# One written list of steps replaced by another in a fused attention and gated-MLP kernel on one Trainium2 core

## The chip, the core and the metric

The kernel runs on one core of a Trainium2 chip. The profile names the engines: PE is TensorE's matmuls and PEld its weight loads, DVE is VectorE, ACT is ScalarE, POOL is GpSimd, SP is SyncE, which here issues all transfers. The metric is device time in microseconds (us); lower is better.

## What is computed

```python
# x: 2048 x 512, all bf16.  The same x feeds both branches.
xn = layernorm(x)                                  # rows, eps 1e-5
# branch A: 32 heads of 16
q, k, v = split(xn @ wqkv)                         # wqkv 512 x 1536
pq, pk  = q @ w_phi[h], k @ w_phi[h]               # 16 x 16 for each head
phi_q   = concat(softmax(pq), softmax(-pq))        # 32 features for each head; phi_k alike
kv, z   = phi_k^T v, sum over tokens of phi_k
o       = (phi_q @ kv) / (phi_q . z + 1e-6)
# branch B: F = 1792
h       = (xn @ w_gate) * (xn @ w_up)
out     = x + o @ wo + h @ w_down
```

## The kernel before

**Data.** x is taken in 16 tiles of 128 tokens, and four tiles make a group of 512. The 1792 hidden columns are 14 chunks of 128. Group 0 goes through plain matmuls. Group 1 goes through gate and up in a seven-product block scheme (Strassen's in Winograd's form) with 256 token columns (the steps with `N` before the name), and groups 2 and 3 together go through the same scheme with 512 columns. For w_down, tiles 9, 10 and 11 are paired with 13, 14 and 15 in that scheme too.

**The order of the work.** A loop builds some 1244 small closures, the steps, each with a name. At the end of the function, one string, `ORDER`, is split into words, and each word's closure is called in turn. What a closure issues is queued on its engine in that order; no scheduler changes it (`manual_schedule`). A word such as `kp7/g` gives the engine of a step that can run on several: `/v` VectorE, `/a` ScalarE, `/g` GpSimd. `SLOTS` says, for each kind of buffer, which of its places each new buffer takes, in the order in which the list asks for them: `s` is for six PSUM banks, `x` for five SBUF buffers, `e` for three exponent tiles. Where a place is asked for again, the step waits until the last reader of its former content is done.

**Turns.** `both_in_sbuf` names the steps all of whose operands are in SBUF. When such a step is called on VectorE, the next step with a GpSimd instruction gets a manual dependency on it: GpSimd waits until VectorE has done it. A VectorE step has no such wait for GpSimd (except `ws`, which waits for the last GpSimd instruction listed ahead of it).

**The steps**, with the lines that the profile shows:

- `g`, `u`: gate and up matmuls of group 0 (L351); `gc` the copy of the gate, `h` the product. `fk`, `fq` fold w_phi into the key and the query weight (L471), `fka fkv fqa fqv` copy the results; `wq` fetches the query weight transposed (L491).
- `s` statistics of a tile on VectorE, `sc` the scaling of four tiles on GpSimd, `a` the normalised tile, `xt` its transposing DMA (L523).
- `vk n.0`, `vk n.1`, `q n.0`, `q n.1`: value, key and query matmuls (L337); `vc` copies the value. `kx ky qx qy` take the exponents on ScalarE (L537), `kr qr` the sums (L549) and `ki qi` the reciprocals (L554) on VectorE, `kp qp` the product on GpSimd (L559). `kv n` adds tile n to the sum over tokens (L590), `kvm` scales that sum (L595), `qt` transposes phi_q by DMA (L616).
- `ab n`: numerators and denominators of the attention (L627); `de` the denominator (L638 on ScalarE), `rd` its reciprocal (L649), `ot` the quotient (L654), `oT` its transposing DMA (L660).
- `f n.i`: products of w_down for tile n (L678; the last two, i = 7 and 8, are with `wo`), `fs` the sum with x, `fo` the store; tile 12 is done in two parts, `f12` and `F12`.
- `n g.k`: a bound on the weights' size on ScalarE (L710); `wr wf wp ws` make powers of two of it; `up` scales the weights with these (L359); `t k i` (L774) and `z i`, `Nz i` (L796) are the differences and sums of weights and tokens that the block scheme needs.
- `p m.b` (L824): the seven products of block b; `k` keeps a partial product (L357), `j` and `d4` join them (`d4` is the direct one), `m` multiplies gate and up (L846).
- `S` (L930), `ct cb wt` (L910): sums for w_down's scheme; `P` its products (L960), `K A B` what is kept and added, `J` the joins (L989), `X t` the store of tile t (L1015).
- `=k`, `=ab`, `=f`, `=ab2` open and close two PSUM banks outside the ring: for the sum over tokens, for the attention, for the narrow blocks (`bank_f`), and for the attention of the last tiles. A pool opens when the last reader of the former one is done.

Of the kernel before, what the change touches and what calls it, by code (L numbers as in the profile page):

```python
# [50 lines left out]
Nk3.2/a j3.2 p2.4 j2.4 p7.3 Np5.2 Np4.2 p2.5 p2.6 k3.3/a Nd4.2/a qi8 j7.3 n2.0 qp8/g Nj7.2 Nm7.1/g p1.5 Np1.3
Nk1.3/a qr13 p3.3 Np3.2 k1.5/a Nj3.2 Np6.3 p6.4 p6.5 Nk2.3/a Np7.3 j2.5 m2.5/g k2.4/a m7.3/v j3.3 Np5.3 Nk3.3/a
up50/a Nj7.3 p7.4 Np2.3 Np4.3 Nd4.3 p5.4 Np3.3 Nm7.3/g Nj2.3 k3.4/a Np1.4 Nk1.4/a p4.3 j7.4 Np2.4 Np6.4 k2.5/a
t23/g Nj3.3 qi13 t30/g Nm2.3/g Nk2.4/a p3.4 j3.4 p7.5 Np7.4 Np1.5 Nj2.4 n2.1 p4.4 d4.3 Nm3.3/v Nk3.4/a t31/v
Np2.5 q10.0 Np4.4 m3.3/g k3.5/a Nk1.5/a p5.5 p4.5 Np6.5 Nj2.5 qi9 j7.5 Nm2.5/g t32/g d4.4/a Nd4.4/a Np5.4 Nj7.4
p1.6 Nk2.5/a Np7.5 Nk3.5/a q10.1 t33/v d4.5 Np3.4 wr2 Nj3.4 wf2 k1.6/a p3.5 Np4.5 up51/a Nd4.5 p6.6 Np1.6
Nk1.6/a Np2.6 qx10 j2.6 k2.6/a qp9/g j3.5 Np5.5 Nj7.5 m7.5/v m3.5/v t40/v t41/g q12.0 p5.6 Np6.6 q12.1 p7.6
Nk2.6/a Np3.5 Np7.6 Nj2.6 Nj3.5 qy10 wp2 qp13/g k3.6/a p1.7 p1.8 Nk3.6/a qx12 k1.7/a Np5.6 Np4.6 p2.7 j7.6 p3.6
p4.6 Nm7.5/g Nd4.6/a oT4 qr10 Nj7.6 Np1.7 qy12 p2.8 p6.7 Np3.6 k1.8/a Nk1.7/a j3.6 k2.7/a Np6.7 j2.7 Nk2.7/a
d4.6/a q14.0 q14.1 Np7.7 Nj3.6 j2.8 Np2.7 p7.7 Nk3.7/a qx14 Np2.9 Nm3.5/v m2.7/v t42/v Nj2.7 k3.7/a Np4.7 qy14  # L60
Np5.7 Nd4.7 p5.7 Nj7.7 t43/g Np2.8 Np1.8 p4.7 Np3.7 j7.7 Nm2.7/g Nm7.7/v Nj3.7 Nm3.7/v Nk1.8/a Np6.8 Nk2.8/a
p1.9 d4.7 p3.7 k1.9/a Np7.8 Np5.8 p6.8 m7.7/g qt13 fo3 qt8 j3.7 p2.9 Nk3.8/a Np4.8 Nd4.8/a k2.8/a p1.10 Nj7.8
Nj2.8 Np3.8 m3.7/g Np1.9 j2.9 Nk1.9/a k1.10/a t50/v ws2 Nj3.8 S1.0/g p6.9 p2.10 Nj2.9 j2.10 Np6.9 p7.8 Np5.9
p5.8 k2.9/a m2.9/v p7.9 Nk2.9/a t52/v k3.8/a j7.8 Np7.9 Nk3.9/a t51/g p5.9 p1.11 p4.8 Nj7.9 p3.8 k3.9/a p4.9
t53/g p6.10 Np4.9 Np3.9 Nm2.9/v j7.9 d4.8/a j3.8 m7.9/g qi10 k1.11/a Nd4.9 p6.11 p3.9 Nj3.9 up61/a t60/v d4.9
Nm7.9/g qp10/g k2.10/a Np1.11 p2.11 j3.9 p7.10 k2.11/a k3.10/a j2.11 Np1.10 p5.10 j7.10 Nm3.9/g m2.11/g m3.9/v
Np2.10 Np2.11 Nk1.10/a Nj2.10 p4.10 p7.11 k3.11/a q15.0 q15.1 S0.3/v qy15 Nk1.11/a d4.10/v p4.11 p3.10 p5.11
Np6.10 qx15 Nk2.10/a p1.12 Nj2.11 Nm2.11/g j3.10 Np6.11 j7.11 t61/g t62/g t63/g Np2.12 Np7.10 p2.12 f6.3 d4.11
m7.11/g k1.12/a oT7 j2.12 Nk3.10/a Np4.10 Nk2.11/a Nd4.10/a f6.1 p3.11 f6.4 qr12 Np7.11 Np5.10 p1.13 ct2.2/a
Nk3.11/a Nj7.10 j3.11 p6.12 fo1 Np3.10 k2.12/a f7.0 Np4.11 k1.13/a p2.13 Nj3.10 S0.5/v j2.13 f7.4 Np1.12 f7.1  # L70
p7.12 cb11.1/a p6.13 Nk1.12/v Nd4.11 Np5.11 f6.8 qi12 Nj7.11 Nj2.12 S1.3/g S2.4/g m3.11/v k3.12/a S0.4/g S1.4/g
Np6.12 q11.0 f6.7 Nk2.12/a ct2.1/a Np7.12 Np3.11 p5.12 qr14 Nj3.11 Nk3.12/a j7.12 Nm3.11/g qp12/g Np4.12 p4.12
Np1.13 q11.1 p3.12 d4.12/a Nd4.12/a m2.13/v Nk1.13/a Np2.13 f7.2 Np5.12 f6.2 Np6.13 f7.8 k2.13/a qr15 j3.12
p7.13 Nj2.13 Nk2.13/a ct1.0/a qi14 Nj7.12 inv1 cb11.0/v qx11 k3.13/a p5.13 Np7.13 f4.2 f4.5 Np3.12 f4.1 Nk3.13/a
p4.13 wt1.0/v Nm2.13/v Nj3.12 Nm7.11/v Np5.13 f7.7 f6.0 qt9 Np4.13 j7.13 qp14/g Nj7.13 Np3.13 d4.13 Nd4.13 p3.13
f4.3 Nj3.13 =ab2 ab8 qy11 ct2.3/g S0.1/v de8/v rd8 ot8 qi15 f4.7 f6.5 f5.2 Nm3.13/g f4.4 f5.0 ct2.0/g ab9 f7.5
S0.2/v Nm7.13/v S2.6/g de9/a rd9 ot9 S2.2/v S2.3/v F12.3 f6.6 f4.8 F12.1 f7.6 wt2.0/v S1.1/g S1.5/g qt14 qt10
qp15/g qt12 m7.13/v oT8 f4.0 j3.13 f7.3 f4.6 F12.2 f5.8 fs4 fs6 ab14 f5.7 de14/a ct1.1/a rd14 oT9 fo0 ot14
S0.6/v m3.13/v f5.1 f5.4 qr11 qi11 f8.8 oT14 f12.5 F12.6 f8.3 fs7 f5.5 f5.3 F12.5 f12.2 ab12 f8.2 P1b.10 de12/a
wt1.1/g wt2.2/g P1a.10 f5.6 f8.7 cb21.0/a f8.5 f8.4 F12.0 K1.10/v S2.1/v rd12 ot12 f12.6 qt15 fo6 P1a.11 f12.1  # L80
ab13 f12.4 P1b.11 oT12 qp11/g fs5 fo7 fo4 fo5 qt11 wt2.1/g ct3.0/a de13/a rd13 ot13 S1.2/v cb22.1/v S1.6/v f8.0
P1a.9 f12.0 P1b.9 f8.1 S3.0/v wt2.3/v S2.5/v wt4.1/v oT13 f12.3 F12.7 f12.7 f12.8 S3.6/v fs12 K1.11/a S2.0/v
ab10 F12.8 ct3.1/a F12.4 cb21.1/a de10/a K1.9/a A1.9/v wt3.1/v P6a.10 f8.6 wt4.0/g P6a.9 P6b.9 K6.9/a cb22.0/a
A6.9/g S3.5/g wt4.3/g S3.4/g P6a.11 P5a.10 P5b.10 Fs12 P6b.10 K6.10/a P2a.9 P2w.9 K5.10/a fs8 P5a.9 rd10 ot10
# [1026 lines left out]
```

## Time and profile before

| | us |
|---|---|
| median of 3 runs | 214.34 (214.32 to 215.28) |
| the profiled execution's own time | 215.05 |
| its span | 213.3 |

A row of the stretches gives, after the stretch and its length, the busy time (us) of TensorE's matmuls, its weight loads, VectorE, ScalarE and GpSimd, each with its count of instructions, then the granted clock, the DMA engines' mean busy share and GB/s. A row of the timeline gives the start, the duration, the engine, the line, the operation with out<-in, the shape, how many instructions are taken together, and in brackets the idle time ahead and what ended it. A matmul of 512 columns is shown with 0.38 us, but such matmuls follow one another every 0.216 us. The mean granted clock of the span is 0.998.

### The profile page before, as it was taken

What the parts mean: (1) busy time and instruction counts of PE and PEld (TensorE: products, weight loads), DVE (VectorE), ACT (ScalarE), POOL (GpSimd) and SP (SyncE); (2) the same over time, 40 slices, a digit from 0 to 9 for tenths busy, and PEclk for the clock granted to TensorE, in tenths of its full rate; (3) what the DMA queues carried; (4) which work ended last, traced back from release to release, by engine and by line L of the source; (5) the groups of instructions that cost most, each with busy time, mean ns of one, the idle gap of its engine ahead of it and who ended that gap; (6) DMA issues with size and microseconds to landing.
All of it is one profiled execution on the core that took longest, in us unless ns stands there. A gap on an engine that the chain in (4) does not pass through costs nothing.

```text
span 213.3 us, 4174 instructions
## 1 busy us (share of the span) xinstructions
PE 206.5 (97%) x1452; PEld 117.8 (55%) x1452; DVE 185.3 (87%) x372; ACT 153.2 (72%) x296; POOL 149.8 (70%) x146
## 2 busy tenths in 40 slices
...
GB/s 158 260 274 383 379 297 177 92 8 33 70 25 77 0 68 105 147 103 77 0 3 0 0 3 32 179 13 3 0 0 0 0 130 119 101 148 75 50 78 74
DMA packets 47253, 19.95 MB, mean 94 GB/s; under 512 B 37504, under 2 KB 46976, under 8 KB 47104
## 3 DMA queue, kind: packets, MB, share of 16 engines
...
q8 instruction: 11, 0.18, 0.4%
q14 instruction: 10, 0.08, 0.2%
HBM read 8.67 MB, written 2.10 MB: 50 GB/s over the span
## 4 chain that ended last, share of the span: by engine, by line
PE 78%; DMA 9%; DVE 6%; SPq 2%; ACT 1%; POOL 1%; issue 1%; DVEq 0%; ACTq 0%; POOLq 0%
PE sa L824 16%; PE fin L678 15%; PE sc L824 9%; PE k L337 5%; PE q L337 5%; PE da L960 5%; PE pv L337 4%; PE sb L824 4%; DMA wT<-in_A_wqkv_dram 3%; PE u L351 3%; DMA wgu<-in_B_w_up_dram 2%; PE g L351 2%; DMA oT<-otok 2%; PE db L960 2%; PE dd L960 2%; PE dc L960 2%
## 5 line engine op out<-in xcount | busy, mean ns | idle before, releaser
L549 DVE TENSOR_REDUCE sums<-e 128x64 f32<-128x1024 f32 x32 | 38.3, 1198 | 3.0 <-ACT e L537 2.9
L559 POOL TENSOR_TENSOR phik<-e,rs 128x1024 bf16<-128x1024 f32 x16 | 30.8, 1935 | 13.8 <-DVE rs L554 10.4
L678 PE MATMUL fin<-wd,hT 128*128 128x512 bf16 (+2 forms) x154 | 37.1, 359 | 0.0
L559 POOL TENSOR_TENSOR phiq<-e,rs 128x1024 bf16<-128x1024 f32 x16 | 31.5, 1975 | 4.8 <-DVE hT L846 2.7
L824 PEld LDWEIGHTS <-T 128*128 128x128 f16 x224 | 21.9, 98 | 17.4 <-issue 0.5
L846 POOL TENSOR_TENSOR hT<-u_sb,hT 128x256 f16<-128x256 bf16 (+1 forms) x23 | 21.1, 920 | 5.3 <-DVE T L774 3.0
L357 ACT COPY k<-sa 128x512 f32<-128x512 f32 (+1 forms) x42 | 19.5, 483 | 5.6 <-PE sa L824 4.1
L359 ACT ACTIVATE k<-sa 128x512 f32<-128x512 f32 (+1 forms) x41 | 19.7, 494 | 4.9 <-PE sa L824 4.2
L824 PEld LDWEIGHTS <-wgu 128*128 128x128 bf16 x168 | 16.3, 98 | 12.3
L337 PEld LDWEIGHTS <-x 128*128 128x128 f16 x144 | 13.4, 98 | 14.4 <-DMA x<-xn 1.1
L678 PEld LDWEIGHTS <-hT 128*128 128x128 f16 (+1 forms) x154 | 14.0, 98 | 11.8
L337 PE MATMUL pv<-vk,x 128*128 128x512 bf16 x48 | 18.2, 379 | 0.8 <-DMA x<-xn 0.8
L351 PEld LDWEIGHTS <-wgu 128*128 128x128 bf16 x128 | 12.0, 98 | 12.0 <-DMA wgu<-in_B_w_up_dram 0.4
L554 DVE RECIPROCAL rs<-sums 128x64 f32<-128x64 f32 x32 | 17.3, 543 | 1.5
L337 PE MATMUL k<-vk,x 128*128 128x512 bf16 x48 | 18.2, 379 | 0.0
L824 PE MATMUL sa<-ss,T 128*128 128x512 f16 x56 | 16.3, 379 | 0.0
L839 DVE SCALAR_TENSOR_TENSOR hT<-sc,k 128x512 f16<-128x512 f32 (+1 forms) x28 | 15.3, 548 | 1.1 <-PE sc L824 0.9
L359 ACT ACTIVATE wgu<-wgu,up 128x1024 bf16<-128x1024 bf16 x14 | 16.0, 1152 | 0.0
L710 ACT ACTIVATE junk<-wgu 128x1024 bf16<-128x1024 bf16 x14 | 15.0, 1077 | 1.2 <-DMA wgu<-in_B_w_gate_dram 1.2
L843 DVE TENSOR_TENSOR u_sb<-sc,k 128x512 bf16<-128x512 f32 (+1 forms) x28 | 15.0, 545 | 0.6 <-PE sc L824 0.5
L537 ACT ACTIVATE e<-q 128x512 f32<-128x512 f32 x24 | 13.9, 601 | 1.9 <-POOL phik L559 1.4
L351 PE MATMUL u<-xnT,wgu 128*128 128x512 bf16 (+1 forms) x64 | 14.6, 352 | 0.1
...
## 6 DMA issues: line engine op xcount, KB each, us to landing
out_dram<-o_sb SPq DMA_DIRECT2D x15, 128.0 KB, 1.9
...
xall<-in_A_x_dram SPq DMA_DIRECT2D x1, 1024.0 KB, 12.1
xall<-in_A_x_dram SPq DMA_DIRECT2D x4, 128.0 KB, 2.5
...
```

Of the source, the lines that this page charges most:

```text
L337: nc.tensor.matmul(ps, lhsT=xt(n)[:, j, :], rhs=w[:, j, :], start=(j == 0), stop=(j == DC - 1))
L351: nc.tensor.matmul(ps, lhsT=w[:, c, f * P:(f + 1) * P], rhs=xnT[:, c, lo:hi], start=(c == 0), stop=(c == DC - 1))
L357: A.copy(out=dst, in_=src)
L359: A.activation(out=dst, in_=src, func=AF.Identity, scale=scale)
L549: V.tensor_reduce(out=sums[:], in_=ev(), axis=AX.X, op=ALU.add)
L554: V.reciprocal(out=rs[:].rearrange("p a b -> p (a b)"), in_=held.pop((s + "s", n))[:])
L559: eng.tensor_tensor(out=phi[:].rearrange("p g (x f) -> p (g x) f", f=DH), in0=ev(), in1=held.pop((s + "i", n))[:].to_broadcast((P, 2 * H, ...
L678: nc.tensor.matmul(held["fin", n, lo], lhsT=l, rhs=r, start=len(done) == 1, stop=len(done) == FC + DC)
L824: nc.tensor.matmul(mine[bankname], lhsT=ww[:, j, :], rhs=xx[:, j, :], start=start and j == 0, stop=(j == hc - 1), skip_group_check=True)
L839: V.scalar_tensor_tensor(out=h(*to), in0=mine[ps], scalar=gate_scale, in1=mine[kept][:], op0=ALU.mult, op1=ALU.add)
L846: eng.tensor_tensor(out=h(*to), in0=mine["u", i][:], in1=h(*to), op=ALU.mult)
L960: nc.tensor.matmul(mine[ps][:, 0:W], lhsT=l, rhs=r, start=bool(mine.pop((ps, "new"), False)), stop=True, skip_group_check=True)
```

## The change

`ORDER` and `SLOTS` are replaced. The new list has the same steps, but that the stores of tiles 13, 14 and 15 come in two halves (`X13.0`, `X13.1` and so on). 96 of the 1244 steps have another engine; among them ten `t` go from VectorE to GpSimd and five the other way, `z1` and `Nz2` from GpSimd to VectorE, four `de` from ScalarE to VectorE, and `de6` and `de8` the other way. By the change's description, each VectorE step on SBUF operands is now listed behind its GpSimd step. The code around it takes a few more general forms (`KN`, a scale for `gate_copy`, another source for `half`), which with `KN = 7` give the same instructions.

The diff, cut to the lists' beginnings and ends and the code:

```diff
 ORDER = """
-g3 gc3/a =k g1 gc1/a fk2 fk0 g0 u3 fkv2/v fkv0/v fka2/a fka0/a k1 ky1 kx1 u0 gc0/v h3 k0 u1 k2 h0 kr1 h1 ki1 kx0
-ky0 kr0 s6 s5 ky2 n1.0 g4 g6 gc4/a u6 g7 n0.5 kx2 gc6/a gc7/a s7 k3 kp1/g s4 sc4 kx3 n1.6 n0.6 ky3 u7 h7 h6 a5/g
-xt5 u4 g12 g11 g13 h4 ki0 u12 g9 u13 a6/g kp0/g gc11/a s9 s11 s10 s8 u11 a4/a xt4 n0.3 gc9/a kr2 gc13/a n0.1 h11
-h13 xt6 wq g10 gc10/a gc12/a kr3 n2.4 u9 h9 ki2 kv0 g5 sc8 a11/g a10/g vk5.0 a8/g xt11 ki3 vk5.1 kp2/g a9/a
-gc5/a a7/a vc5/a s13 h12 kx5 vk4.0 vk4.1 vc4/a kp3/g vk6.0 s14 fq0 xt10 s15 s12 sc12 xt8 xt9 xt7 ky4 kx4 ky5
-fqa0/v vk6.1 ky6 kv1 g2 fq2 kv2 kx6 kr4 ki4 kr6 ki6 fqv0/a fqv2/a kp4/g u5 kv3 vk7.0 vk7.1 kr5 kp6/g vc6/a gc2/a
-n1.3 fqa2/a ky7 vk8.0 vk8.1 kv4 kx7 ki5 h5 u2 kr7 ki7 n1.4 kp5/g vc8/a kx8 ky8 a12/a vk10.0 vk10.1 vc7/a ky10
-kx10 a13/a kp7/g h2 vk9.0 kv5 kr8 ki8 kp8/g kv6 xt12 vk9.1 ky9 vc10/a kx9 n0.4 q0.0 q0.1 a15/v kr10 vk11.0
-vk11.1 ky11 ki10 kx11 kv7 kv8 vk12.0 q1.0 q1.1 kp10/g xt13 a14/v kr9 ki9 kp9/g vc11/a vc9/a xt14 Nz0/v qy0 qx0
-kr11 ki11 qr0 qi0 g8 gc8/a qy1 u10 qx1 kp11/g n0.0 kv9 vk13.0 vk12.1 kv10 qr1 h10 xt15 ky12 kx12 qp0/g qi1
-vk13.1 qp1/g kr12 ki12 qt0 kv11 vk14.0 vc13/a vc12/a kx13 ky13 kr13 ki13 vk15.0 vk14.1 u8 vk15.1 h8 kp12/g
-kp13/g z0/v n0.2 kx14 ky14 n1.5 kr14 q3.0 q5.0 kv12 vc15/a ki14 ky15 kx15 kp14/g qt1 q2.0 kr15 ki15 n1.1 kp15/g
-f3.1 q2.1 qx2 q3.1 f3.2 kv13 q5.1 f3.4 qy2 f3.0 f2.1 f2.0 qr2 qi2 qp2/g vc14/a kv14 f1.2 f1.3 f2.4 z2/v qx5 n2.2
-qy5 n1.2 kv15 qx3 qy3 kvm0 kvm1 =ab qr5 q4.0 f1.0 f1.6 ab1 n2.6 wr0 f2.2 de1 wf0 qt2 rd1 qi5 ot1 wp0 q6.0 q6.1
-q7.0 q7.1 f1.4 f2.3 qx6 oT1 ws0 qr3 ab0 qy6 de0 qi3 qp5/g n2.3 up00/a qr6 rd0 up01/a qt5 f0.1 f1.5 f0.4 q4.1 qi6
-f2.6 f0.3 f2.5 f0.5 f1.1 qp3/g ot0 qx4 qy4 ab2 f1.8 qr4 up41/a qy7 qx7 qp6/g de2 qi4 f1.7 rd2 fs1 ot2 qt3 oT0
-qp4/g q9.0 f3.5 q9.1 q8.0 q8.1 f0.2 qr7 z1/g inv0 ab3 qt6 oT2 up21/a de3 qi7 rd3 f3.3 ot3 qx9 qt4 t00/v t02/v
-Nz1/v f0.8 up20/a qy9 qp7/g p1.1 f0.7 p1.0 qx8 qy8 k1.1/a Nz3/g k1.0/a ab5 de5/a up11/a f0.6 p2.0 f0.0 t01/v
-p6.0 k2.0/a rd5 ot5 n2.5 up60/a f2.7 ab6 t03/g j2.0 f2.8 p7.0 de6/v k3.0/a oT3 f3.8 fs0 rd6 ot6 p2.1 p6.1 oT5
-qt7 oT6 fs2 ab4 j2.1 fo2 z3/g de4/a rd4 ot4 k2.1/a q13.0 q13.1 qr8 p5.0 up10/a j7.0 t10/g Nz2/g p4.0 d4.0/a p7.1
-Np2.1 ab7 de7/a f3.6 p5.1 f3.7 k3.1/a rd7 ot7 qy13 p4.1 p3.0 =f fs3 Np1.1 up31/a Nk1.1/a Np1.0 Nk1.0/a p2.3
-Np6.1 qx13 j3.0 Np6.0 p2.2 Nj2.1 Nk2.1/a j7.1 d4.1 Nk2.0/a up30/a t11/g m2.1/g Np2.0 Nj2.0 t12/g p3.1 j3.1 Np7.0
-Np7.1 Nk3.1/a Nk3.0/a p1.2 k1.2/a p1.3 qr9 m7.1/g Np4.1 Np4.0 Nd4.0/a p5.2 t13/v Np5.0 up40/a Nd4.1 p6.2 Nj7.0
...
-ab15 wt3.0/v P7a.9 P5b.9 P8w.10 fo12 fo8 oT10 Fo12 K5.9/a de15/v wt4.2/v P7b.9 P2b.9 J2.9 rd15 ot15 K7.9/a
-P7a.10 P7b.10 P4w.9 P6b.11 S3.1/g K7.10/v P3b.9 P4a.9 P4b.10 P4w.10 ab11 B6.9/v A7.10/g oT15 K6.11/a A1.10/v
-A7.9/g A6.11/g P7a.11 P4a.10 P4b.9 S3.3/v J8.10 S3.2/v A6.10/g J4.10 J4.9 P7b.11 P5a.11 P8w.9 J8.9 P3w.9 K7.11/a
-P3a.9 P4a.11 P2b.10 de11/a rd11 ot11 X14 oT11 J3.9 X9 B6.10/g P3a.11 P4b.11 P2w.10 P4w.11 P5b.11 X13 P2a.10
-P3w.10 J2.10 K5.11/a P3b.10 A7.11/v B6.11/g J4.11 A1.11/v P3w.11 P8w.11 J8.11 X15 P3b.11 J3.11 P2b.11 P3a.10
-J3.10 X10 P2a.11 P2w.11 J2.11 X11
+g3 gc3/v =k g1 gc1/a g0 gc0/a fk2 fk0 fkv0/v u3 u1 u0 h0 h1 fkv2/a fka0/a fka2/a h3 n0.1 k0 k2 kx0 ky0 k3 kr0
+kx2 k1 g4 u4 ky2 kr2 g6 ki0 g7 kx3 ky3 gc4/a n0.4 gc6/a gc7/a s7 s5 s4 s6 kp0/g u6 ky1 g13 g2 ki2 kx1 u7 n1.0
+n0.6 sc4 a5/a kr1 g11 h6 ki1 h4 h7 s11 a4/g xt4 kp1/g a6/g u12 g12 gc13/a n1.6 gc12/a xt6 xt5 gc11/a kp2/g s8
+h12 n1.4 s10 s9 g9 u9 gc9/a u13 u11 g5 u2 a7/g xt7 h13 n2.6 h9 n0.0 vk4.0 kr3 s13 gc5/a gc2/a vk4.1 kv0 vk5.0
+s12 vk5.1 sc8 a11/a a10/g ky4 ki3 a8/g vc4/a kx4 a9/a vc5/a kx5 ky5 s15 s14 vk6.0 kp3/g vk6.1 ky6 wq kx6 n2.3
+kr4 ki4 h11 kr6 h2 kv1 u10 g10 kv2 kv3 u5 vc6/a sc12 ki6 kr5 xt10 xt8 kp4/g a15/g kp6/g gc10/a a12/a n0.2 vk7.0
+h10 vk7.1 kx7 ky7 ki5 vk8.0 vk8.1 fq2 h5 vc7/a xt12 xt9 xt11 kr7 ki7 kx8 kp5/g fqa2/a ky8 a14/a kv4 vk10.0
+vk10.1 kp7/g xt14 kv5 kv6 vk9.0 kx10 ky10 fqv2/v kr8 ki8 kr10 fq0 vc8/a ki10 kp8/g fqa0/a vk9.1 a13/a kv7 vk11.0
+ky9 kx9 vk11.1 fqv0/v vc9/a kx11 ky11 vc10/a kp10/g kr9 ki9 kp9/g q0.0 kr11 ki11 q1.0 q0.1 q1.1 kv8 g8 xt15
+vk12.0 xt13 Nz0/v qy0 qx0 gc8/a kv9 kv10 vk12.1 qr0 qi0 kp11/g qx1 qy1 n1.2 qp0/g vc12/a vc11/v kx12 ky12 vk13.0
+n0.3 vk13.1 qr1 vk15.0 kv11 vk15.1 kx13 ky13 qi1 qp1/g vc13/a kr12 ki12 kp12/g n1.3 vk14.0 vc15/v kr13 qt0 ki13
+vk14.1 q3.0 f1.3 f1.0 q5.0 q5.1 ky14 kx14 kr14 kv12 vc14/a q2.0 q2.1 u8 ki14 qt1 kx15 ky15 kp13/g n0.5 kp14/g
+f3.6 f1.2 kr15 h8 qy2 qx2 ki15 f3.1 f3.2 f3.0 q7.0 q7.1 kv13 kv14 n1.5 f1.5 kp15/g qr2 qi2 qp2/g kv15 qx5 qy5
+n1.1 wr0 f0.2 q3.1 n2.5 qr5 kvm0 kvm1 wf0 qi5 =ab ab1 de1 rd1 ot1 qx3 qy3 qt2 f2.3 wp0 ws0 qp5/g f1.6 f1.1 f0.0
+qr3 qx7 qy7 n2.0 up01/a oT1 ab0 q6.0 q6.1 qy6 de0 qi3 f0.6 f3.3 inv0 up00/a f1.4 f2.1 f0.5 z0/v qp3/g f1.8 q8.0
+qx6 qt3 f0.3 f1.7 rd0 qr7 ot0 q8.1 ab2 f2.5 t00/g qr6 de2 up30/a up10/a up31/a t02/g qi7 rd2 q4.0 q4.1 qx4 qi6
+ot2 qy4 n2.2 f3.4 f0.1 f2.4 f2.6 f0.4 oT0 f0.7 t01/g z1/v n2.4 ab3 qp6/g p1.0 qp7/g k1.0/a fs1 f0.8 p1.1 qr4
+f2.0 qy8 k1.1/a qt5 de3 fs0 oT2 rd3 qi4 ot3 q13.0 p6.0 f3.5 q13.1 qx8 qr8 p2.0 n2.1 qt6 oT3 qp4/g j2.0 p6.1 qt4
+ab5 de5/v k2.0/a qx13 k2.1/a z2/v up21/a qy13 f2.7 p2.1 f2.8 f2.2 rd5 ot5 p7.1 oT5 z3/g fs2 j2.1 t03/g ab6 de6/a
+rd6 p7.0 ot6 p5.1 qt7 wr2 wf2 q9.0 fo2 oT6 k3.1/a up11/a k3.0/a f3.7 Nz2/v Nz1/v j7.1 ab4 de4/a rd4 ot4 p5.0
+j7.0 p4.1 p4.0 p3.1 up41/a d4.0/a f3.8 ab7 up51/a t10/g de7/v wp2 up20/a p1.2 q9.1 rd7 ot7 p3.0 j3.1 =f fo0
+Np1.0 j3.0 d4.1 Np1.1 fs3 Nk1.0/a t11/g Nz3/g m2.1/g Nk1.1/a m7.1/g Np6.0 Np2.1 Nk2.0/a p2.2 Np7.0 k1.2/a j2.2
+Np6.1 p1.4 Np2.0 Nk3.0/a Np4.0 p2.3 qy9 Nj2.1 t12/v Nk2.1/a ws2 Np7.1 Nd4.0/a Np5.0 Nj7.0 Nk3.1/a qx9 p6.2 Np4.1
...
+P4w.10 qp11/g de10/v rd10 ot10 oT10 S3.5/v P7b.9 P5b.10 ab15 P2w.9 fs8 fo8 qt11 K5.10/v P4a.10 K7.9/a de15/v
+rd15 wt4.2/g P4b.10 A7.10/g J4.10 ot15 P5a.9 P5b.9 P4b.9 P8w.10 P4w.9 S3.1/g P3a.9 A1.9/g J2.9 A1.10/v X14.0
+J8.10 P3b.10 P3w.9 K5.9/a P4a.9 P3b.9 P6b.11 P2a.11 J4.9 A6.10/g X14.1 oT15 A6.9/g A7.9/g ab11 de11/v rd11 ot11
+oT11 P2w.10 P3a.10 B6.9/g P2a.10 P2b.11 P3w.10 P2b.10 P8w.9 B6.10/g K6.11/a A6.11/v J3.10 P5a.11 J3.9 A1.11/v
+X13.0 X9 J8.9 X13.1 P7a.11 P7b.11 P5b.11 K7.11/v K5.11/a B6.11/g J2.10 P3a.11 P3w.11 P2w.11 J2.11 P3b.11 J3.11
+X11 X10 P8w.11 A7.11/g J8.11 X15.1 P4w.11 P4a.11 P4b.11 J4.11 X15.0
 """
...
@@ -348,7 +348,7 @@
     def half(w, name, T, f, lo, hi):
         ps = bank(name)[:, 0:hi - lo]
         for c in range(DC):
-            nc.tensor.matmul(ps, lhsT=w[:, c, f * P:(f + 1) * P], rhs=xnT[:, c, lo:hi],
+            nc.tensor.matmul(ps, lhsT=w[:, c, f * P:(f + 1) * P], rhs=(x4 if T else xnT)[:, c, lo:hi],
                              start=(c == 0), stop=(c == DC - 1))
         return ps
@@ -362,9 +362,9 @@
         else:
             eng.tensor_scalar(out=dst, in0=src, scalar1=scale, scalar2=None, op0=ALU.mult)
-    def gate_copy(ps, n, eng=A):
+    def gate_copy(ps, n, eng=A, scale=None):
         g_sb = ring(gpool, "g", [P, TT], BF16, "g_sb")
-        copy(eng, g_sb[:, 0:n], ps)
+        copy(eng, g_sb[:, 0:n], ps, scale)
         return g_sb
     def hidden(T, f, ps, g_sb, lo, hi):
@@ -428,6 +428,10 @@
     inv2 = consts.tile([P, 2], F32)
     steps = {}
     held = {}
+    KN = 7
+    levels = (8.0, 8.0, 4096.0)
+    hidden_scale = 16.0
+    gate_scale = hidden_scale / (levels[0] * levels[1])
     def step(name, default=None):
         def add(fn):
@@ -444,7 +448,7 @@
         @step(f"gc{u}", A)
         def _(eng):
-            held["gc", u] = gate_copy(held.pop(("g", u)), TT - lo, eng)
+            held["gc", u] = gate_copy(held.pop(("g", u)), TT - lo, eng, gate_scale if T else None)
         @step(f"u{u}")
         def _():
@@ -454,7 +458,7 @@
         def _():
             hidden(T, f, held.pop(("u", u)), held.pop(("gc", u)), lo, TT)
-    for u in range(FC):
+    for u in [*range(FC), *(FC + k + i for i in (0, FH) for k in range(KN, FH))]:
         unit_steps(u)
     def fold_steps(name, qk, dst, j0):
@@ -695,9 +699,6 @@
     fro = consts.tile([P, 3], F32)
     up3 = consts.tile([P, 3], F32)
     down3 = consts.tile([P, 3], F32)
-    levels = (8.0, 8.0, 4096.0)
-    hidden_scale = 16.0
-    gate_scale = hidden_scale / (levels[0] * levels[1])
     def pair_cols(k):
         return wgu[:].rearrange("p g c (h f) -> p g c h f", h=2)[:, :, :, :, k * P:(k + 1) * P]
@@ -872,7 +873,8 @@
     for b in range(2 * FH):
         block_steps(b, 0)
-        block_steps(b, 1)
+        if b < 2 * KN:
+            block_steps(b, 1)
     W = D // 2
     quarters = {11: wd[:, 0:FH, 0:W], 12: wd[:, 0:FH, W:D], 21: wd[:, FH:FC, 0:W], 22: wd[:, FH:FC, W:D]}
@@ -1011,8 +1013,12 @@
         join(8, m, 1, "d", lambda: kept("k3"))
         product(4, "a", a(3, FH), d("t4"), False, (m, 0))
         join(4, m, 0, "a", lambda: x(m, 0))
-        for t in (n, m):
-            steps[f"X{t}"] = (lambda t=t: nc.sync.dma_start(out=out_view(t, t + 1)[:, 0, :], in_=mine["o", t][:]), None)
+        def store(t, lo, hi):
+            nc.sync.dma_start(out=out_view(t, t + 1)[:, 0, lo:hi], in_=mine["o", t][:, lo:hi])
+
+        steps[f"X{n}"] = (lambda: store(n, 0, D), None)
+        for c in range(2):
+            steps[f"X{m}.{c}"] = (lambda c=c: store(m, c * W, (c + 1) * W), None)
     t0 = 1
     LAST = 12
```

100 lines of the change are left out of this document (50 added, 50 removed).

## The prediction

> **What bounds the kernel now.** I read the page's first part and the chain that ended last, then the busy time of each engine in stretches of 5 us, then the timeline wherever TensorE sat idle.
>
> ```profile
> span 213.3 us, 4174 instructions
> PE 206.5 (97%) x1452; PEld 117.8 (55%) x1452; DVE 185.3 (87%) x372; ACT 153.2 (72%) x296; POOL 149.8 (70%) x146
> PE 78%; DMA 9%; DVE 6%; SPq 2%; ACT 1%; POOL 1%; issue 1%; DVEq 0%; ACTq 0%; POOLq 0%
> ...
> 35.00:40.00 5.00, 4.74 (x44) 2.22 (x42) 4.86 (x12) 4.69 (x10) 4.91 (x5) 1.00 0.84 135
> 40.00:45.00 5.00, 4.15 (x47) 2.13 (x46) 4.69 (x7) 4.36 (x9) 4.77 (x5) 1.00 0.31 62
> ...
> 70.00:75.00 5.00, 4.44 (x34) 2.00 (x33) 4.79 (x7) 3.57 (x8) 4.45 (x3) 1.00 0.00 0
> 75.00:80.00 5.00, 4.99 (x39) 2.46 (x38) 4.85 (x13) 4.87 (x10) 3.77 (x4) 1.00 0.38 72
> ...
> 90.00:95.00 5.00, 4.28 (x31) 1.84 (x28) 3.88 (x10) 4.97 (x8) 4.84 (x6) 1.00 0.76 96
> 95.00:100.00 5.00, 5.00 (x40) 2.59 (x38) 4.82 (x9) 3.82 (x9) 3.83 (x3) 1.00 0.55 119
> ...
> 205.00:210.00 5.00, 5.00 (x47) 4.34 (x45) 3.18 (x7) 0.47 (x1) 0.72 (x1) 1.00 0.32 93
> 210.00:213.30 3.30, 0.11 (x2) 0.00 (x0) 0.48 (x1) 0.00 (x0) 0.00 (x0) 0.89 0.28 98
> ```
>
> The second column of a window is TensorE's busy time, the next ones weight loads, VectorE, ScalarE and GpSimd. TensorE is the bound: 206.5 of 213.3 us, and its clock is whole in every stretch that works. The same matmuls run after the change, so only the 6.8 us of idle time can be won: 0.26 + 0.85 in 35 to 45 us, 0.56 in 70 to 75, 0.72 in 90 to 95, 3.19 behind the last matmul. About 1.2 us lie in the first 10 us, ahead of the list and untouched. From 95 to 210 us there is next to nothing to win. A new list can therefore gain about 2.5 us at most, and lose without a limit. Near the bound stand VectorE (4.7 to 5.0 of 5 us through most of it) and, up to 100 us, ScalarE.
>
> The four waits, in the timeline:
>
> ```profile
> 38.34 0.41 PE L471 MATMUL pq<-bd,wT 64*128 64x64 bf16 x16 [0.26 <-DMA wT<-in_A_wqkv_dram]
> 43.51 0.39 PE L337 MATMUL pv<-vk,x 128*128 128x512 bf16 x1 [0.85 <-DMA x<-xn]
> 72.54 0.43 PE L590 MATMUL kv<-vt,phik 128*128 128x68 bf16 x8 [0.39 <-POOL phik L559]
> 74.43 0.43 PE L590 MATMUL kv<-vt,phik 128*128 128x68 bf16 x8 [0.17 <-POOL phik L559]
> 94.24 0.61 PE L678 MATMUL fin<-wo,oT 128*128 128x512 bf16 x2 [0.72 <-DMA oT<-otok]
> ```
>
> These are steps `fq0`, `vk7.0`, `kv14`, `kv15` and `f3.8`.
>
> **The change, part by part.** Every step keeps its work; the list, the engine of 96 of the 1244 steps and the buffers' places change. `KN = 7` adds nothing: 7 is `FH`, so the extra loop is empty and every block keeps both groups.
>
> *Transposes of x and of the query weight.* SyncE issues in order:
>
> ```profile
> 26.71 5.08 SPq L523 DMA_TRANSPOSE x<-xn  x3
> 31.84 2.92 SPq L491 DMA_TRANSPOSE wT<-in_A_wqkv_dram  x1
> 34.85 21.09 SPq L523 DMA_TRANSPOSE x<-xn  x9
> ```
>
> Before, `xt7` is the eighth x transpose, behind the long `wq` (2.92 us of issue), and TensorE wants it right behind `kv3`. After, `xt4 xt6 xt5 xt7` go first, `wq` comes fifth, and `fq2` and `fq0` stand behind `vk8` and `vk9`. Both waits (1.11) should go. Late next would be `vk8.0`, on `xt8`, two issues behind `wq` as `xt10` was. I take the gain of 1.1; the other end is 0, if the statistics (`s7 s5 s4 s6`, moved behind two sums) bring `xt4` late.
>
> *The end of the keys.* VectorE stood in the way of `kv14`:
>
> ```profile
> 64.22 3.83 POOL L559 TENSOR_TENSOR phik<-e,rs 128x1024 bf16<-128x1024 f32 x2
> 66.50 2.10 DVE L796 TENSOR_TENSOR ss<-x 128x1024 f16<-128x1024 f16 x1
> 70.55 3.83 POOL L559 TENSOR_TENSOR phik<-e,rs 128x1024 bf16<-128x1024 f32 x2 [2.50 <-PE q L337]
> 73.76 1.16 DVE L796 TENSOR_TENSOR ss<-x 128x1024 f16<-128x1024 f16 x1
> 74.84 0.77 DVE L595 TENSOR_TENSOR KV<-kv,M 128x272 bf16<-128x272 f32 x2
> ```
>
> `z0` (66.50) takes 2.10 us on VectorE ahead of the sums of tile 14, and GpSimd, which must also wait for it by the list's turn, stands 2.50 us idle. After, `z0` and `z2` (3.3) stand behind the attention's begin; two parts of `W1q` and two value copies (0.6 each) come to VectorE instead of some smaller steps, so that up to `kv15` it has 71 steps instead of 73 and 2.8 us less to do. I take all 0.56 as won. Against it: `ab1` now stands two steps (`f0.2`, `q3.1`) behind `kv15` instead of three, with `qr5` listed ahead of the two scalings of 0.77. Two steps give 0.86 us; the scalings and their latency need about 1.2. I charge 0.3, between 0 and 1.2 (`qr5` just begun).
>
> *From attention to the first blocks.* Before, `oT3` waits behind `oT2` on SyncE and `f3.8` stands 6.1 us of TensorE work behind `ab3`. After it is 11.2 us: the 0.72 go. New short places: `de6` goes to ScalarE, ahead of `ab4`; `Np1.0`, the first step in the bank pool that opens when `ot7` is done, stands three pairs behind `ab7` (1.3 us) instead of five (2.2). The chain, from rows of before:
>
> ```profile
> 98.18 0.42 PE L627 MATMUL ab<-KV,phiqT 128*128 128x68 bf16 x8
> 98.63 0.38 ACT L638 ACTIVATE den<-ab,eps,inv 128x32 f32<-128x32 f32 x1 [0.19 <-PE ab L627]
> 99.30 0.34 DVE L649 RECIPROCAL rden<-den 128x32 f32<-128x32 f32 x1
> 99.73 0.69 DVE L654 TENSOR_TENSOR otok<-ab,rden 128x512 bf16<-128x512 f32 x1
> ```
>
> From the end of `ab7` (98.60) to that of `ot7` (100.42) it is 1.8 us with ScalarE's 0.38; with VectorE's own `de7` about 1.6. So `Np1.0` waits 0.35. For `ab4` and `ab7` I charge 0.35 together, between 0 and the price of the ScalarE rival.
>
> *VectorE and GpSimd.* 64 VectorE steps on SBUF operands instead of 69; ten differences `t` go to GpSimd, five come back:
>
> ```profile
> 98.03 1.16 POOL L774 TENSOR_TENSOR T<-wgu 128x512 f16<-128x512 bf16 x1 [1.17 <-ACT wgu L359]
> 89.33 0.75 DVE L774 TENSOR_TENSOR T<-wgu 128x512 f16<-128x512 bf16 x2
> ```
>
> A `t` takes 1.16 us there and about 0.4 here. TensorE waits for GpSimd nowhere but at `kv14` and `kv15`, and in the quoted stretches GpSimd works 3.77 and 3.83 of 5 us: that idle time hides the moved steps, and I cost them at nothing. Without the cover a late `t` costs its 1.16.
>
> A page of the Trainium skill speaks against this part: "SBUF — State Buffer", section "Who interferes with whom", says that a VectorE operation with two SBUF inputs and a GpSimd operation that reads SBUF exclude one another, and that the later to start is blocked until the other ends. The trace agrees: `z0` began under a GpSimd product that ran to 68.05 and ended 0.54 behind it. By that rule being listed behind a GpSimd step removes no wait; it only says who waits, and by it alone this part is worth nothing.
>
> *The stores.*
>
> ```profile
> 209.51 0.60 PE L960 MATMUL db<-wo,oT 128*128 128x256 bf16 x4
> 210.15 0.48 DVE L989 SCALAR_TENSOR_TENSOR o_sb<-db,inv,dK 128x256 bf16<-128x256 f32 x1 [0.39 <-PE db L960]
> 205.39 5.60 SPq L1015 DMA_DIRECT2D out_dram<-o_sb  x5
> out_dram<-o_sb SPq DMA_DIRECT2D x15, 128.0 KB, 1.9
> out_dram<-o_sb SPq DMA_DIRECT2D x1, 32.0 KB, 1.7
> ```
>
> The last store is now 64 KB instead of 128; these rows bound the landing by 1.7 and 1.9. Three more issues of 0.34 lie on an otherwise idle queue. Gain 0.1, between 0 and 0.2.
>
> **The sum:** -1.11 - 0.56 - 0.72 - 0.1 = -2.5 won; 0.3 + 0.35 + 0.35 = 1.0 given back; -1.5 net. The profiled execution took 215.05 us, of which its span is 213.3; it would take 213.6, span 211.8. It lies 0.7 above the median of 214.34, on which scale I forecast **212.9 us**, with 212.2 to 213.6 its own range.
>
> **Rivals.**
>
> 1. *ScalarE is late at the attention's end: slower.* Between `kv15` and `de4` the old list gives ScalarE 12 exponents, 3 norms, 7 weight scalings, 4 keeps and 2 `de`; the new one 14, 6, 7, 6 and 2.
>
> ```profile
> L357 ACT COPY k<-sa 128x512 f32<-128x512 f32 (+1 forms) x42 | 19.5, 483 | 5.6 <-PE sa L824 4.1
> L710 ACT ACTIVATE junk<-wgu 128x1024 bf16<-128x1024 bf16 x14 | 15.0, 1077 | 1.2 <-DMA wgu<-in_B_w_gate_dram 1.2
> L537 ACT ACTIVATE e<-q 128x512 f32<-128x512 f32 x24 | 13.9, 601 | 1.9 <-POOL phik L559 1.4
> 72.51 0.60 ACT L537 ACTIVATE e<-q 128x512 f32<-128x512 f32 x1 [1.43 <-POOL phik L559]
> 96.05 0.38 ACT L638 ACTIVATE den<-ab,eps,inv 128x32 f32<-128x32 f32 x1 [0.98 <-ACT k L359]
> ```
>
> Two exponents (1.2), three norms (3.2) and two keeps (1.2, at the 0.60 of the wide form) are 5.6 us more, while TensorE has four pairs (1.7) more: 3.9 net. ScalarE's own slack there was 1.43 + 0.98 = 2.4. What is left is 1.5 us, unless ScalarE enters the stretch that much earlier relative to `kv15`: from there it decides. The new list gives it two exponents (1.2), a norm (1.1) and a copy less ahead of `kv15`, 2.6 us, which speaks against this rival; its exponents wait for TensorE's banks and GpSimd's products, which may eat the lead. Then `ab4` and `ab7` are late by 1.5 and the earlier gains vanish in that wait: 214.34 + 1.5 = **215.8**.
>
> 2. *VectorE takes ScalarE's part: no change.* Its stretch from `kv15` to `d4.1` gets `z0`, `z1`, `z2` (2.10, midway 1.63, and 1.16: 4.9) and loses three `t` (1.2); the rest of the two lists differs by 0.3: 4.0 us more. Its idle time in three of the stretches shown was 0.15 + 1.12 + 0.18 = 1.45. If the other 2.55 use up its lead of 2.8, `d4.1` ends as late as now: **214.3**.
>
> 3. *Nothing new waits:* the whole 2.5, **211.9**. Against it speak the three short distances named above.
>
> 4. *The blocked pair decides: slower.* `z0`, `z1`, `z2` all run on VectorE now, where GpSimd is fullest. Each may wait for a whole GpSimd product (1.94, half of 3.83) and then run 0.6: 2.5 each, 7.6 instead of the 4.9 counted. Rival 2 leaves 0.25 us of lead, so this costs 2.7 - 0.25 = 2.4: **216.8**. It decides once more than one of the three is blocked. The page named above has this as its rule; the row of `z0` bears it out once in two.
>
> That the list does not do what it says (the waits stay where they are because the engines are late anyway) ends as rival 2.
>
> **How the numbers follow.** Forecast 0.46, rival 1 0.20, rival 2 0.18, rival 3 0.08, rival 4 0.08. About 0.5% (1.07 us) is what a measurement of this kernel can tell from no change, so faster means below 213.3. Of the forecast's 0.46, 0.38 lie below it, with rival 3's 0.08: faster 0.46. Same: 0.08 + 0.15 of rival 2 = 0.23. Slower: 0.20 + 0.08 + 0.03 = 0.31. The range goes from 211.6, past rival 3, to 216.0, past rival 1; rival 4 and the ends of the unknown costs beyond it are the 2 in 10 left out.
>
> **What would show it.** Right: no idle time of TensorE at `vk7.0`, `fq0`, `kv14`, `kv15` and `f3.8`; short waits at `ab1`, `ab4` and `Np1.0`; a tail of 3.1 to 3.2 us behind the last matmul. Rival 1: TensorE idle at `ab4` or `ab7` for over 1 us, ScalarE without idle time from 74 to 97 us. Rival 2 and 4: VectorE at 5.0 there, `z1` near 2 us or more. The whole is wrong if TensorE waits by more than 1 us in the first 50 us (the statistics moved late) or anywhere behind 105 us, where I expect nothing.

## The result, and the profile after

| | us |
|---|---|
| before, median of 6 runs beside the changed kernel | 214.63 (214.24 to 215.28) |
| changed, median of 6 runs | 213.36 (213.23 to 213.42) |
| ratio | 0.9938, 95% interval 0.9919 to 0.9956 |
| changed, the profiled execution: its own time / its span | 213.42 / 211.7 |
| changed, once more in a later comparison (12 runs beside 23 of before) | 213.28 beside 214.01, ratio 0.9969 (0.9953 to 0.9986) |

The changed kernel is faster by 0.6% in the first comparison and by 0.3% in the second. Its own times hardly differ between the two; those of the kernel before lie, over all comparisons, anywhere from 212.98 to 215.47. What makes them differ is part of the answer.

The page of the changed kernel, its first part:

```profile
span 211.7 us, 4173 instructions
PE 205.6 (97%) x1452; PEld 117.7 (56%) x1452; DVE 183.8 (87%) x373; ACT 152.3 (72%) x292; POOL 150.1 (71%) x149
```

The stretches that answer to those of before (the second column is TensorE's busy time, then weight loads, VectorE, ScalarE, GpSimd):

```profile
35.00:40.00 5.00, 5.00 (x39) 2.51 (x38) 4.76 (x12) 4.56 (x10) 4.57 (x5) 1.00 1.11 136
40.00:45.00 5.00, 5.00 (x42) 2.54 (x39) 4.38 (x7) 4.82 (x9) 4.68 (x6) 1.00 0.12 25
70.00:75.00 5.00, 5.00 (x53) 2.84 (x52) 4.70 (x10) 4.58 (x11) 4.59 (x4) 1.00 0.00 0
85.00:90.00 5.00, 4.90 (x32) 2.26 (x31) 4.93 (x9) 4.80 (x11) 5.00 (x3) 1.00 0.86 132
90.00:95.00 5.00, 4.89 (x45) 2.44 (x44) 4.88 (x12) 4.56 (x8) 3.81 (x3) 1.00 0.54 107
95.00:100.00 5.00, 4.18 (x32) 1.97 (x29) 4.14 (x9) 4.12 (x6) 4.42 (x6) 1.00 0.53 125
100.00:105.00 5.00, 4.70 (x35) 3.14 (x33) 4.76 (x14) 4.47 (x11) 3.17 (x4) 1.00 0.00 0
```

TensorE's idle time from 35 to 45 us (1.11 before), at 70 to 75 (0.56) and most of that at 90 to 95 (0.72) is gone. A new loss stands at 95 to 105 us: 0.82 + 0.30. The timeline there, first TensorE's rows, then VectorE's, then SyncE's:

```profile
99.64 0.61 PE L825 MATMUL sa<-x,wgu 128*128 128x256 f16 x4 [0.82 <-DVE otok L658]
100.55 0.38 PE L825 MATMUL sa<-s,T 128*128 128x256 f16 x2 [0.30 <-ACT k L359]
...
97.85 0.35 DVE L653 RECIPROCAL rden<-den 128x32 f32<-128x32 f32 x1
98.89 0.69 DVE L658 TENSOR_TENSOR otok<-ab,rden 128x512 bf16<-128x512 f32 x1 [0.69 <-DMA oT<-otok]
...
93.56 1.26 SPq L620 DMA_TRANSPOSE phiqT<-phiq  x1
94.92 0.53 SPq L696 DMA_DIRECT2D out_dram<-o_sb  x1
95.54 1.19 SPq L664 DMA_TRANSPOSE oT<-otok  x1
```

The rows are read from the top. `Np1.0`, the first step of the pool `=f`, waits for `ot7`. `ot7` has its reciprocal at 98.20, yet begins 0.69 us later: not for an engine, but for a DMA that reads `otok`. The quotients have two places in `SLOTS` (`ot`), `ot7` takes the one that `ot6` had, and its reader is the transpose `oT6`. On SyncE this stands behind `qt7` and the store `fo2`, is issued at 95.54 and lands at 98.80 (the chain of waits gives it 3.26 us). Behind it the chain is that quotient, one keep on ScalarE, and then almost only TensorE.

### The profile page after: what moved, and what is told of

Read it like the earlier page. It is cut to its first block, busy times and chain, and to the rows that moved or that the text cites. A ratio compares the mean times of both kernels' runs of the same rounds, so it can differ in the third digit from the quotient of the medians.

```text
span 211.7 us, 4173 instructions
## 1 busy us (share of the span) xinstructions
PE 205.6 (97%) x1452; PEld 117.7 (56%) x1452; DVE 183.8 (87%) x373; ACT 152.3 (72%) x292; POOL 150.1 (71%) x149
## 4 chain that ended last, share of the span: by engine, by line
PE 51%; DMA 2%; DVE 1%; ACT 0%; issue 0%; ACTq 0%; DVEq 0%
PE sa L825 15%; PE fin L682 11%; PE sc L825 8%; PE da L962 5%; PE sb L825 4%; PE q L337 2%; PE dd L962 2%; PE db L962 2%; PE dc L962 2%; DMA oT<-otok 2%; PE ab L631 1%; DVE otok L658 0%; DVE o_sb L991 0%; ACT k L359 0%; ACTq L359 0%
## 5 line engine op out<-in xcount | busy, mean ns | idle before, releaser
L682 PE MATMUL fin<-wd,hT 128*128 128x512 bf16 (+2 forms) x154 | 36.4, 360 | 0.0
L563 POOL TENSOR_TENSOR phiq<-e,rs 128x1024 bf16<-128x1024 f32 x16 | 30.9, 1936 | 7.3 <-DVE hT L847 2.5
L847 POOL TENSOR_TENSOR hT<-u_sb,hT 128x512 f16<-128x512 bf16 (+1 forms) x20 | 18.1, 913 | 5.6 <-DVE down L740 1.8
L775 POOL TENSOR_TENSOR T<-wgu 128x512 f16<-128x512 bf16 x12 | 13.8, 1160 | 5.2 <-PE sc L825 2.1
L359 ACT ACTIVATE wgu<-wgu,up 128x1024 bf16<-128x1024 bf16 x14 | 15.8, 1153 | 0.0
L541 ACT ACTIVATE e<-k 128x512 f32<-128x512 f32 x24 | 13.4, 606 | 1.3 <-PE k L337 1.2
```

What stands on the lines that cost most here:

```text
L359: A.activation(out=dst, in_=src, func=AF.Identity, scale=scale)
L563: eng.tensor_tensor(out=phi[:].rearrange("p g (x f) -> p (g x) f", f=DH), in0=ev(), in1=held.pop((s + "i", n))[:].to_broadcast((P, 2 * H, ...
L682: nc.tensor.matmul(held["fin", n, lo], lhsT=l, rhs=r, start=len(done) == 1, stop=len(done) == FC + DC)
L847: eng.tensor_tensor(out=h(*to), in0=mine["u", i][:], in1=h(*to), op=ALU.mult)
```

## The experiments

"Idle time" below is that in brackets ahead of a matmul. Every ratio is to the kernel before in the same comparison.

**A place of its own for `ot7`** (changed kernel; `vt0` is a value buffer that is not used after `kv15`):

```diff
-            t = held["ot", n] = ring(dpool, "ot", [P, D], BF16, "otok")
+            t = held["ot", n] = (vpool.tile([P, D], BF16, name="otok", tag="vt0", bufs=1) if n == 7
+                                 else ring(dpool, "ot", [P, D], BF16, "otok"))
-    "ot": "0101010101001010",
+    "ot": "010101001001010",
```

> The changed kernel, but the quotient of tile 7 (ot7) gets a buffer of its own. Theory: in the changed kernel ot7 waits 0.69 us until the transposing DMA oT6 has read the place that it reuses, and with it the pool =f and Np1.0. Then ot7 starts at the end of its reciprocal, TensorE's idle time ahead of Np1.0 falls from 0.82 to about 0.2 us, and the time falls by 0.6 to 0.7 us (ratio to before about 0.990 to 0.991). Rival: VectorE or ScalarE is late there anyway and the wait only moves to the next keep (no change, ratio 0.9938).

Measured: 212.43 us (212.12 to 212.85), ratio 0.9922 (0.9894 to 0.9950). The timeline of this kernel:

```profile
98.28 0.69 DVE L659 TENSOR_TENSOR otok<-ab,rden 128x512 bf16<-128x512 f32 x1
99.03 0.61 PE L826 MATMUL sa<-x,wgu 128*128 128x256 f16 x4 [0.16 <-DVE otok L659]
99.94 0.38 PE L826 MATMUL sa<-s,T 128*128 128x256 f16 x2 [0.30 <-ACT k L359]
```

The quotient begins behind its reciprocal, and 0.82 has become 0.16: 0.66 us. The place was the cause of that wait. Against the changed kernel's later comparison the time is 0.85 lower, of which the trace accounts for the 0.66; the two ratios' intervals lie just apart (0.9950 and 0.9953), while that of the first comparison overlaps. This run and the next, which cannot be told from it, are the fastest of the study.

**The same, with `Np6.0` behind `Np2.1`:**

```diff
-Nk1.1/a m7.1/g Np6.0 Np2.1 Nk2.0/a
+Nk1.1/a m7.1/g Np2.1 Np6.0 Nk2.0/a
```

> As the run before, and Np6.0 listed behind Np2.1 instead of ahead of it. Theory: Np6.0 writes the bank that the keep Nk1.0 reads, and one pair (0.43 us) is too short for that keep; behind two pairs the 0.30 us of idle time ahead of it goes too: 1.0 to 1.1 us below the changed kernel (ratio to before about 0.989). Rival: the join Nj2 or the next keep is then what TensorE waits for, and nothing is won over the run before.

Measured: 212.47 us, ratio 0.9924 (0.9894 to 0.9953): the rival. The 0.30 us ahead of `Np6.0` are no longer one wait, but nothing is won: from the start of `Np1.0` to the next matmuls of 512 columns on `x` and `wgu` it is 2.21 us without the swap (99.03 to 101.24) and 2.19 with it (98.40 to 100.59). Small gaps between the groups of matmuls take the place of the wait.

**`xt7` early in the list before:**

```diff
-fq0 xt10 s15 s12 sc12 xt8 xt9 xt7 ky4
+fq0 xt7 xt10 s15 s12 sc12 xt8 xt9 ky4
```

> The kernel before, but xt7 issued ahead of xt10 instead of as the last of four. Theory: vk7.0's wait of 0.85 us goes, vk8.0 has its x in time, and since every engine has slack up to kv14 the gain reaches the end: 0.7 to 0.9 us less (ratio about 0.996). Rival: VectorE sets the pace up to kv14 (4.7 to 5.0 of 5 us busy), so the time won is lost again in a longer wait at kv14: ratio 0.999 to 1.001.

Measured: 213.45 us beside 214.01, ratio 0.9975 (0.9955 to 0.9994). The idle time ahead of `vk7.0` is gone and `kv14` waits 0.38 as ever, so nothing is lost again there; the gain is about 0.5 us, under the 0.7 to 0.9 expected, which the interval still allows. The 0.72 ahead of `f3.8` were missing too, though nothing was moved there. That asked for another execution of the kernel before.

**The kernel before again,** unchanged, one execution:

> The kernel before itself, for a second look at its waits. Theory: vk7.0, kv14 and kv15 wait in every execution, 0.85 and 0.56 us. f3.8's 0.72 us hang on how SyncE's transposes fall in that execution, and may be missing. Rival: f3.8 waits as long again, and it was xt7 that took that wait away in the run with xt7 early.

Measured: 213.34 us, where the profiled execution of the prediction took 215.05. Its timeline has these waits in place of the five quoted there:

```profile
37.92 0.41 PE L471 MATMUL pq<-bd,wT 64*128 64x64 bf16 x16 [0.19 <-DMA wT<-in_A_wqkv_dram]
71.35 0.43 PE L590 MATMUL kv<-vt,phik 128*128 128x68 bf16 x8 [0.38 <-POOL phik L559]
73.24 0.43 PE L590 MATMUL kv<-vt,phik 128*128 128x68 bf16 x8 [0.17 <-POOL phik L559]
```

and its stretches:

```profile
40.00:45.00 5.00, 4.85 (x50) 2.50 (x50) 4.64 (x7) 4.60 (x10) 4.84 (x5) 1.00 0.21 43
90.00:95.00 5.00, 4.95 (x37) 2.28 (x36) 4.79 (x10) 4.75 (x9) 5.00 (x4) 1.00 0.45 86
```

Of `vk7.0`'s 0.85 us at most 0.15 are left in its stretch, of `f3.8`'s 0.72 at most 0.05; `fq0` waits 0.19 instead of 0.26, and `kv14` and `kv15` wait as before. The time from issue to landing of the one transpose `qt4`, issued at 88.11 in the profile of the prediction:

```profile
phiqT<-phiq SPq DMA_TRANSPOSE x1, 4.9
```

and in this execution, issued at 86.90:

```profile
phiqT<-phiq SPq DMA_TRANSPOSE x1, 3.2
```

The same transpose, in the same place of the same list, took 1.7 us longer to land in one execution than in the other, and `oT3`, on which `f3.8` waits, stands right behind it on SyncE (4.7 us to landing, then 3.3). So the expectation held but for `vk7.0`: it had been taken for a steady wait, and is another that hangs on transposes. There SyncE took 2.11 us to issue `xt10` in the first profile and 1.42 in the second, and everything behind it in the queue, `xt7` too, came later by as much.

What makes one transpose slow was not tried, but the traces hold a lead. In each of the three profiles of the old list and its variants in which `qt4` takes 4.7 to 5.1 us (the first one, `xt7` early, and the third run with late sums below), a load of instructions of 0.02 MB, on DMA queue q8, starts just before its issue or while it is under way: at 90.6, 86.8 and 89.3 us, for issues at 88.11, 86.95 and 88.25. In the four others `qt4` takes 3.2 to 3.6 us, and the load starts some 1.5 us ahead of its issue or behind its landing (in the second execution at 90.5, where `qt4` lands at 90.1). This is a coincidence in time; no run moved the load.

**`z0` and `z2` late in the list before,** alone, with `z1` on VectorE, and with `t01` early:

```diff
-kp13/g z0/v n0.2 ... f2.4 z2/v qx5 ... f0.4 q4.1 ... k1.0/a ab5
+kp13/g n0.2 ... f2.4 qx5 ... f0.4 z0/v q4.1 ... k1.0/a z2/v ab5
 second run, besides:
-qr7 z1/g inv0
+qr7 z1/v inv0
 third run, z1 on GpSimd:
-t00/v t02/v Nz1/v ... qp7/g ... f0.0 t01/v
+t00/v t02/v t01/v Nz1/v ... qp7/g ... f0.0
```

> The kernel before, but z0 and z2 listed behind the beginning of the attention. Theory: the waits at kv14 and kv15 (0.56 us) go and the sums find room behind them: 0.4 to 0.6 us less (ratio about 0.9975). Rival: VectorE is full up to 100 us, so the 3.3 us moved make f3.8, ab4 or Np1.0 late instead: ratio 1.000 or above, up to 1.005.

> The kernel before with z0 and z2 listed late, as in the run that cost 1.2%, and z1 on VectorE as well. Theory: there TensorE waited 2.2 us for z1, which ran 2.13 us on GpSimd, and what stood behind it in the turns; on VectorE z1 takes 0.7 to 1.6 us, that wait goes, and the time is 0.3 to 0.6 us below before (ratio 0.997 to 0.9985). Rival: VectorE is full there, and z1 on it pushes the quotients ot1 to ot3 back: ratio 1.003 to 1.010.

> The kernel before with z0 and z2 late (as in the run that cost 1.2%), and t01 moved from behind qp7 to right behind t02, ahead of it. Theory: in the two runs with late sums it was neither z1 nor a full VectorE that cost 2.2 us at p6.0, but t01, which began 0.2 to 0.4 us after the GpSimd product qp7, took 2.15 us instead of 0.41 and ended with it; ahead of qp7 the turn makes GpSimd wait instead, t01 takes 0.4 us, TensorE's 2.2 us go, and the ratio to before falls from 1.011 to 0.999 to 1.002 (the 0.5 us at ab2 and 0.2 to 0.4 us at ab3 stay). Rival: VectorE is late there by its load, p6.0 waits as long as before for z1 or t01, and the ratio stays over 1.007.

Measured: ratios 1.0117 (1.0079 to 1.0154), 1.0107 (1.0075 to 1.0140) and 1.0020 (0.9999 to 1.0041). In all three the waits at `kv14` and `kv15` are gone, as forecast. In the first two the time is lost again, and more, at `p6.0`; the timeline of the first, GpSimd, VectorE, TensorE:

```profile
90.01 2.21 POOL L559 TENSOR_TENSOR phiq<-e,rs 128x1024 bf16<-128x1024 f32 x1
90.35 2.15 DVE L774 TENSOR_TENSOR T<-wgu,T 128x512 f16<-128x512 bf16 x1
92.56 0.89 PE L824 MATMUL sa<-ss,T 128*128 128x512 f16 x2 [2.19 <-DVE T L774]
```

`t01` began 0.34 us after GpSimd's product `qp7`, and took 2.15 us instead of 0.41: it ended 0.28 us behind it. The sums themselves were not late, so the second of these, which blamed `z1`, missed; in it `p6.0` still waits 1.87 us for `t01`. The third, which to the first only adds `t01` listed ahead of `qp7`, took the 2.19 away:

```profile
89.29 0.41 DVE L774 TENSOR_TENSOR T<-wgu,T 128x512 f16<-128x512 bf16 x1
```

The wait itself is not the whole loss of the first two. Behind it TensorE's granted clock falls below 1.00, as it does in these two profiles alone up to 208 us; the stretch of the first:

```profile
92.50:96.50 4.00, 3.72 (x17) 1.76 (x19) 3.15 (x7) 2.76 (x5) 4.00 (x3) 0.57 0.28 55
```

In the second the clock is 0.51 from 94.0 to 97.5, in the third, without the wait, 1.00 throughout. Four us at 0.57 are an estimated 1.7 us more. It does not come every time: of the first run's six executions three have a mean clock of 0.992 (217.06 us and more) and three of 1.00 (216.39 and less).

The third still does not win over before: `ab3` now waits 0.32 us for its transpose and `ab6` 0.71, until just behind the end of tile 5's quotient (91.68), and `f3.8` had 0.82 in that execution. (The expectation names `ab2` and `ab3` for the waits that stay; the trace has them at `ab3` and `ab6`.) Late sums alone do not win their 0.56 in the old list.

**Without the turns,** in the changed kernel and in the one before:

```diff
         if on_dve and both_in_sbuf.match(name):
-            turn = on_dve[-1]
             if name.startswith("ws") and pool_last is not None:
```

> The changed kernel without the turns (a GpSimd step no longer waits for the VectorE step on SBUF operands listed ahead of it). Theory: the turns keep VectorE from being blocked; without them more VectorE steps on SBUF operands start under a GpSimd step and end with it, z0 and z1 up to 2.5 us each, and the time rises by 0.5 to 2 us. Rival: the list keeps them apart by itself, since each stands behind its GpSimd step, and the time stays within 0.3 us.

> The kernel before without the turns. Theory: in both lists it is the turns that keep VectorE from being blocked by GpSimd, so this loses about what the changed kernel lost without them (10.8 us): ratio 1.04 to 1.06. Rival: the new list's order of GpSimd step first, VectorE step behind it, is made for the turns, and the old list loses much less without them: ratio under 1.025.

Measured: 224.04 us, ratio 1.0477 (1.0453 to 1.0501), and 221.23 us, ratio 1.0355 (1.0326 to 1.0384). One group of VectorE's products in the changed kernel, and the same group without turns:

```profile
L847 DVE TENSOR_TENSOR hT<-u_sb,hT 128x256 f16<-128x256 bf16 (+1 forms) x22 | 7.4, 352 | 0.1
```

```profile
L847 DVE TENSOR_TENSOR hT<-u_sb,hT 128x256 f16<-128x256 bf16 (+1 forms) x22 | 15.1, 700 | 0.1
```

The same 22 instructions take twice as long. The page's line of busy times without turns:

```profile
PE 208.0 (94%) x1430; PEld 117.1 (53%) x1452; DVE 199.6 (90%) x373; ACT 153.4 (69%) x292; POOL 153.3 (69%) x149
```

VectorE's busy time grows from 183.8 to 199.6 us with the same instructions, and the program by 10.8. Both expectations were too small, or wrong in form: the changed kernel lost five times the upper end of "0.5 to 2 us", and the kernel before lost 7.3 us, between the two ranges that I had given. The new list leans on the turns more than the old (10.8 us against 7.3). What its order would be worth with all else equal was not separated.

**Whole stores,** in the changed kernel:

```diff
-            steps[f"X{m}.{c}"] = (lambda c=c: store(m, c * W, (c + 1) * W), None)
+        steps[f"X{m}"] = (lambda: store(m, 0, D), None)
```

(with one `X` behind the later half in the list.)

> The changed kernel with the second tiles' stores whole again. Theory: the span's end behind the last matmul is longer by 0.1 us (0 to 0.2), so the time is that of the changed kernel within 0.2 us. Rival: three issues fewer on SyncE shorten it, and it is faster by up to 0.2 us.

Measured: 213.41 us (212.98 to 213.66) beside 213.28 (213.08 to 213.57) for the changed kernel, in the same comparison:

> The changed kernel itself, once more, beside the next three. Theory: the four waits that it takes away are waits in every execution, so the ratio to before stays near 0.994, and the idle time ahead of Np1.0 and of the step behind it is again 0.8 and 0.3 us. Rival: f3.8's wait in the kernel before depends on how the transposing DMAs fall in that execution (it was missing in the run with xt7 early), and the ratio moves by 0.3% from chip to chip.

The times do not tell the two apart. The traces do: with halves the last join of that execution starts at 208.26 and the span ends at 211.3, with whole stores at 208.43 and 211.7. From one to the other that is 3.04 us with halves and 3.27 whole: about 0.2 us, the upper end of the forecast. In that run of the changed kernel the two new waits were 0.82 and 0.30 again: they are steady, unlike most of those that they replace. The ratio did move, as the rival had it.

**Two more short distances,** on top of the place of its own:

```diff
-qt5 de3 fs0 oT2 ... z3/g fs2 j2.1 t03/g ab6 de6/a rd6 p7.0 ot6 p5.1
+qt5 fs0 de3 oT2 ... z3/g j2.1 t03/g ab6 de6/a rd6 p7.0 ot6 fs2 p5.1
```

> The changed kernel with a buffer of its own for ot7, fs0 listed ahead of de3 and fs2 behind ot6. Theory: the waits that are left are short list distances on VectorE: q13.0 waits 0.26 us for the bank that fs0 frees, and ab4 waits 0.27 us for ot6, with fs2 (0.74 us) ahead of it. Each move takes most of its wait away: 0.3 to 0.5 us below the kernel with the place alone (ratio to before 0.988 to 0.991). Rival: VectorE has no room there (4.9 of 5 us), each move only hands the wait to the next user of VectorE, and the ratio is that of the place alone, about 0.992.

Measured: 213.69 us beside 213.97, ratio 0.9984 (0.9967 to 1.0001): worse than the place alone, for a reason that neither theory had. The timeline:

```profile
94.71 0.17 PE L725 MATMUL nrm<-nrm,const-bfloat16-1.0 128*128 128x7 bf16 x1 [1.43 <-DVE o_sb L692]
```

`fs2` frees the PSUM bank that `wr2` takes next; moved behind `ot6`, it holds TensorE for 1.43 us, where 0.27 were to be saved.

## Why the prediction was right, and where it was not

The forecast was 212.9 on the scale of a median of 214.34, a gain of 1.5; measured are 1.3 in the first comparison and 0.7 in the second. The profiled executions themselves went from 215.05 to 213.42, 1.6 less, where the sum gave 213.6. The waits that were to go went, and the net is right; but that it came so close is in part luck. The profiled execution that the sum starts from was a slow one of its kernel (215.05, where a second took 213.34), and the 214.63 of the first comparison lies above the 213.92 to 214.01 of the four later ones; in the one of these that holds the changed kernel, half of the forecast gain is left. Several terms were wrong, in opposite directions.

| term of the sum | forecast | the profile after |
|---|---|---|
| `fq0` and `vk7.0` | -1.11 | gone |
| `kv14` and `kv15` | -0.56 | gone |
| `f3.8` | -0.72 | gone |
| the last store | -0.1 | -0.1 (last join to end: 3.15 to 3.06) |
| `ab1` behind the two scalings | +0.3 | no wait |
| `ab4`, `ab7` | +0.35 | 0.11 in 90 to 95 us, where `ab4` lies |
| `Np1.0` and the step behind it | +0.35 | +1.12 |
| 85 to 90 us | nothing | +0.10 |
| the first 10 us | nothing | +0.45 (1.15 to 1.60 us idle, for a fetch of weights; 0.96 in the second profile of the changed kernel) |

The last column adds up to -0.7, which is what TensorE's idle time lost (6.8 to 6.1 us). The other 0.9 us of the 1.6 are in its busy time (206.5 to 205.6) with the same matmuls. A matmul of 512 columns is drawn 0.38 us long and the next can follow after 0.216, so waits up to about 0.16 us count as busy time; whether the 0.9 are such waits is not shown.

*The waits won.* All are gone, as the forecast had it: the transposes of x stand ahead of `wq`, the sums behind the attention's beginning, `oT3` further from `f3.8`. But I took one execution's waits for the kernel's. Of the 2.39 us, `kv14` and `kv15` (0.56) wait in all four traces of the old list that leave `z0` and `z2` in their places, `fq0` keeps 0.19 of its 0.26 in the second execution, while `vk7.0` and `f3.8` vary with the transposing DMAs. (The prediction had `oT3` late behind `oT2`; the rows have it behind `qt4`, and both landing late.) Two executions of the same program are 1.7 us apart, most of it those waits (1.11 + 0.72 against 0.34 + 0.05). That would explain why the gain is smaller beside the quicker executions. That the changed kernel repeats within 0.5 us fits its readers standing further from those DMAs; no run tested that.

*The price.* "So `Np1.0` waits 0.35" failed. The chain over `ab7`, `de7`, `rd7` and `ot7` was right: with a place of its own for `ot7` the wait is 0.16. What I left out is that `ot7`'s place must be free, on a path through SyncE: `oT6` had been moved behind the store `fo2`. The list shows it, but I followed engines and values there, not buffers. How much of that path is the store was not tried: its issue begins 0.62 us ahead of `oT6`'s, and the wait is 0.69. The 0.30 of the keep I missed as well; the swap shows that a longer distance at that one place does not win it back.

*The overpriced terms.* `ab1` does not wait; the trace shows TensorE busy for all of 70 to 75 us:

```profile
72.24 0.42 PE L594 MATMUL kv<-vt,phik 128*128 128x68 bf16 x8
72.57 0.79 DVE L599 TENSOR_TENSOR KV<-kv,M 128x272 bf16<-128x272 f32 x2
73.41 0.41 PE L631 MATMUL ab<-KV,phiqT 128*128 128x68 bf16 x8
```

The first scaling reads only the first bank of the sum, and begins while `kv15` (72.24) is still drawn; both scalings are done at 73.36. From the end of `kv15` to `ab1` it is 0.75 us, where the prediction counted 1.2, and `qr5` was out of the way.

*The rivals.* ScalarE did not decide: it waited for TensorE where this rival had TensorE wait for it, as the timeline of `de6` shows:

```profile
92.85 0.38 ACT L642 ACTIVATE den<-ab,eps,inv 128x32 f32<-128x32 f32 x1 [0.44 <-PE ab L631]
```

VectorE's load cost at most the 0.10 and 0.11 of 85 to 95 us, the only idle time of TensorE from 70 to 95; `z0`, `z1`, `z2` took 1.00, 1.60 and 0.68 us, 3.3 in all, where 4.9 were counted:

```profile
77.36 1.00 DVE L797 TENSOR_TENSOR ss<-x 128x1024 f16<-128x1024 f16 x1
83.12 1.60 DVE L797 TENSOR_TENSOR ss<-ss,x 128x1024 f16<-128x1024 f16 x1
90.59 0.68 DVE L797 TENSOR_TENSOR ss<-x 128x1024 f16<-128x1024 f16 x1
```

The blocked pair did not decide in the changed kernel, but its mechanism was the right one to fear: with one step beside the wrong product it cost 2.19 us in the kernel before with late sums. The Trainium skill ("SBUF — State Buffer", section "Who interferes with whom") has this as a rule, that the later of the two to start is blocked until the other ends. `t01`'s 2.15 us, and the 352 ns that become 700 without turns, agree with it. The forecast's reading of the rule, that a place in the list alone removes no wait, leaves out the turns, which decide on which side the wait falls: GpSimd with its idle time, or VectorE with none.
